# Input in seven plain pieces a batch, outputs stored in row order of their making, one load queue, last chunk in four tiles of 128

## The chip, the cores and the metric

The kernel runs on one core of a Trainium2 chip. Its engines each work through their own list of instructions in order: TensorE (PE, matrix products), VectorE (DVE), ScalarE (ACT), GpSimd (POOL) and SyncE (SP, which only issues transfers). The metric is the device time of one execution in microseconds. Times here are us unless marked ns.

## The reference

Eight batches of 3136 rows with 256 columns go through the real part of a two-dimensional Fourier transform, then through one block with layer norm, two weight matrices, ReLU and a residual.

```python
X = np.fft.fft(np.fft.fft(x, axis=1), axis=2).real          # x: (8, 3136, 256), fp32
mu, var = X.mean(-1), X.var(-1)
xn = (X - mu) / sqrt(var + 1e-6) * g_ln
out = X + np.maximum(xn @ w_ch1, 0) @ w_ch2                 # w_ch1: (256, 1024), w_ch2: (1024, 256)
```

The weights arrive as float64.

## The kernel before

**Fourier transform along the rows.** The input is real, so row k and row 3136-k of the result come from the same two sums, a cosine part a and a sine part b: row k is a+b, row 3136-k is a-b. Only 1569 values of k are computed per batch; k = 0 and k = 1568 have no partner. The length is split as 64 times 49. For each batch, `fold_zw` (L220) adds input rows n and 3136-n into z and w for one of seven pairs of slots, `step1` (L267) multiplies by the 64-point table, ACT copies the product to `s1`, and `store1` (L287) writes it to a scratch tensor in DRAM. `relayout` (L292) reads the scratch back with the other index on the partitions, and `step2` (L308) multiplies by the second table. In batch 0 the folds run on DVE and the products in plain fp32; in batches 1 to 7 the folds run on POOL, two values hi and lo stand for one fp32, and three passes (hi hi, hi lo, lo hi) stand for one product.

**The block.** `step2` leaves the transform along the rows in chunks of 256 values of k (all batches in one line: 49 chunks, the last with 264), as `ck` and its halves `ckh` and `ckl`. The second transform is folded into the first weight matrix. For each chunk there are eight stages s, one per 128 of the 1024 hidden columns: `moe1_a` (L350) makes a and b of the hidden value in PSUM with 6 matmuls; ACT copies a to `asb`; DVE forms `h` = a+b and a-b side by side (512 columns); `moe1_b` (L375) makes the ReLU hi on ACT (`h_hi`) and lo on DVE (`h_lo`); `moe2` (L429) adds 12 matmuls into `acc` for two tiles of 128 rows, both signs. `residual` and its two followers (L454 to L497) make X itself and its variance, `finish` (L514) joins them and `store_out` (L529) writes the rows.

**Order.** PE, ACT, DVE and POOL run in the order in which the program is written, SP too up to the loop. The part ahead of the loop (L719 to L844) is written out by hand; the loop runs `moe1_b(s-1)`, `moe1_a(s)`, late work, `moe2(s-3)`, further work, for s = 6 to 391, with the Fourier work of the next batch put at numbered stages by `add` and `add_late` (L653 to L705).

**Input.** The rows n of a batch go to `x1` by plain loads on 64 partitions each (`load_x`, L182), the rows 3136-n to `x2` by an indirect gather with an index per partition (`gather_x`, L176), issued by POOL. Batch 0 has its own loads on three queues (L725 to L737). Batch 1 is loaded by POOL ahead of the loop (L783 to L785), every further batch in one place of the loop (L691). One partition range of `x2` is cleared by `clear_x`.

**Weights.** Each quarter of a weight matrix is 128 x 512 float64 values; `convert_m`, `convert_z`, `convert_b` (L566 to L590) turn it to fp32 with four DVE instructions and one on ACT, `finish_w1` or `finish_w2` adds one. For w1, `transform_w1` multiplies by the table `tw_s` on PE and `split_w1` makes `w1_hi` on ACT and `w1_lo` on DVE; `split_w2` makes `w2_hi` on ACT and `w2_lo` on POOL.

**Output.** A row k and its partner lie far apart in the output. So `store_out` scatters the a-b half of each tile with an indirect store on POOL (L421) and writes the a+b half with two to four strided stores on SP (`rows`, L540). In the last chunk a third tile of 64 rows, `tail`, holds the 8 columns over 256, both signs (L440 to L444, L518 to L523).

**Stretches without work for PE** are partly filled by matmuls on zeros (`warm_up`, L711).

Of the kernel before, what the change touches and what calls it, by code (L numbers as in the profile page):

```python
# [42 lines left out]
def unit_k(unit):  # L43
    if unit == 0:
        return np.concatenate([64 * np.arange(25), 32 + 64 * np.arange(25)])
    return unit + 64 * np.arange(49)


def runs():

    out, t = [], 0
    for g in range(16):
        for unit in (g, 16 + g):
            if unit == 0:
# [12 lines left out]
def tables():  # L67
# [19 lines left out]
    for g in range(16):  # L87
        for q in range(2):
            k = unit_k(g + 16 * q)
            n = len(k)  # L90
            for par, v in vs:
                al = 2 * np.pi * ((v[:, None] * k) % N) / N
                c, s = np.cos(al), np.sin(al)
                m = len(v)
                for comp in range(2):
                    rows = tab[par, comp, q, :m]
                    if n == 50:
                        half = slice(25 * comp, 25 * comp + 25)
                        rows[:, 0, half], rows[:, 1, half] = c[:, half], s[:, half]
                        tz[2 * par + comp, :m, half] = c[:, half]  # L100
# [19 lines left out]
    tabs["idx"] = index_table()  # L120
# [3 lines left out]
def index_table():  # L124

    idx = np.zeros((128, 2 * NB + 2 * NCH + 1), np.int32)
    rev = 63 - np.arange(64)
    for b in range(NB):
        for j in range(2):
            idx[:64, 2 * b + j] = (b * 64 + rev) * 7 + 5 + j  # L130
            idx[64:, 2 * b + j] = (b * 64 + rev) * 7 + 3 + j
    k = np.concatenate([k0 + 64 * np.arange(n) for _, n, k0 in runs()])
    spare = iter(range(NB * N, ROWS))
    plus = [b * N + i for b in range(NB) for i in k]
    minus = [next(spare) if i in (0, N // 2) else b * N + N - i for b in range(NB) for i in k]
# [9 lines left out]
def tile_kernel(ctx: ExitStack, tc: tile.TileContext, x, g_ln, w1, w2, tu, tab, tz, ty, tw, idx, out):  # L145
# [11 lines left out]
    idx_s = const.tile([128, 2 * NB + 2 * NCH + 1], I32, name="idx_s")  # L157
    idx0 = const.tile([128, 2, 2], I32, name="idx0")
# [7 lines left out]
    x1 = const.tile([128, NS, D], F32, name="x1")  # L166
    x2 = const.tile([128, NS, D], F32, name="x2")
# [3 lines left out]
    spacer = const.tile([128, 1], F32, name="spacer")  # L171

    xv = x.rearrange("b (u v) d -> b u v d", v=49)
    xg = x.rearrange("b (m r) d -> (b m) (r d)", r=7)

    def gather_x(b, j):  # L176
        ix = idx0[:, b, j:j + 1] if b < 2 else idx_s[:, 2 * b + j:2 * b + j + 1]
        nc.gpsimd.indirect_dma_start(
            x2[:, 7 * j:7 * j + 7].rearrange("p s d -> p (s d)"), None, xg,
            bass.IndirectOffsetOnAxis(ap=ix, axis=0))  # L180

    def load_x(b, j, eng=nc.sync):  # L182
        p0 = 7 - 7 * j
        in_order(eng.dma_start(x1[0:64, p0:p0 + 7], xv[b, :, 1 + p0:8 + p0]))
        if p0 == 0:
            in_order(eng.dma_start(x1[64:128, 0:7], xv[b, :, 15:22]))
        else:
            in_order(eng.dma_start(x1[64:128, 7:10], xv[b, :, 22:25]))
            in_order(eng.dma_start(x1[64:128, 10:11], xv[b, :, 0:1]))

    def clear_x(eng=nc.gpsimd):

        eng.memset(x2[64:128, 3:4], 0.0)

    def load_batch(b):
        for j in (1, 0):
            gather_x(b, j)
            load_x(b, j)

    def slots(p0, p1):  # L200
        stop = NS - 1 - p1
        return x1[:, p0:p1], x2[:, NS - 1 - p0:(stop if stop >= 0 else None):-1]
# [17 lines left out]
    def fold_zw(b, i, eng):  # L220
# [5 lines left out]
        a, c = slots(2 * i, 2 * i + 2)  # L226
# [75 lines left out]
    def width(c):  # L302
        return LASTW if c == NCH - 1 else CW

# [3 lines left out]
    def step2(m, part, of=None):  # L308
# [15 lines left out]
        t = b * HALF + base  # L324
        stop = b * HALF + end
        while t < stop:
            c = min(t // CW, NCH - 1)
            n = min(stop, c * CW + width(c)) - t
# [5 lines left out]
            src = ps[:, :, t - b * HALF - base:t - b * HALF - base + n]  # L334
# [10 lines left out]

    def hcols(c):

        return 2 * CW if width(c) == CW else LASTW + 32 + CW

    def moe1_a(s, passes=((0, 1), (1, 0), (0, 0))):  # L350
# [16 lines left out]
        h = hh[s] = work.tile([128, hcols(c)], F32, tag="h", name=f"h{s}", bufs=4)  # L367
        nc.scalar.copy(asb[:, :w], pa)  # L368
        nc.vector.tensor_tensor(out=h[:, :w], in0=asb[:, :w], in1=pb, op=ALU.add)  # L369
        if w > CW:  # L370
            nc.vector.tensor_tensor(out=h[:, w:w + 32], in0=asb[:, w - 32:w], in1=pb[:, w - 32:w],
                                    op=ALU.subtract)
        nc.vector.tensor_tensor(out=h[:, -CW:], in0=asb[:, :CW], in1=pb[:, :CW], op=ALU.subtract)  # L373

    def moe1_b(s):  # L375
        h = hh[s]
        n = hcols(s // 8)
# [7 lines left out]
    def toks(c):  # L385
        t = [(0, 0), (128, 128)]
        if width(c) > CW:
            t.append((LASTW - 32, CW))
        return t

    def tail(i):

        return i == 2

    def previous(engine):
        return next((i for i in reversed(nc.cur_bb.bb.instructions) if i.engine == engine), None)

    stores = []

    def stored(issue, engine):  # L400


        before = previous(engine)
        again = any(i is before for i in stores)
        if again and engine == mybir.EngineType.Pool:
            nc.gpsimd.memset(spacer, 0.0)  # L406
        dma = issue()
# [13 lines left out]
    def scatter(ix, o):  # L421
        stored(lambda: nc.gpsimd.indirect_dma_start(  # L422
            out, bass.IndirectOffsetOnAxis(ap=ix, axis=0), o, None), mybir.EngineType.Pool)

# [4 lines left out]
    def moe2(s, tiles=(0, 1, 2)):  # L429
# [3 lines left out]
        for i, (t0, _) in enumerate(toks(c)):  # L433
            if i not in tiles:
                continue
            if f == 0:
                acc[c, i] = psum.tile([128, 2, D], F32, tag="y" if tail(i) else f"acc{c % 2}",
                                      name=f"acc{c}_{i}", bufs=1 if tail(i) else 2)
            if tail(i):
                for n, (wi, xi) in enumerate(PASSES):  # L440
                    nc.tensor.matmul(acc[c, i][:64, 0], hs[xi][:, t0:t0 + 64], ws[wi][:, f],
                                     start=(f == 0 and n == 0), stop=(f == 7 and n == 2),
                                     skip_group_check=True)
                continue  # L444
            for side in range(2):
                h0 = t0 + side * (hcols(c) - CW)
                for n, (wi, xi) in enumerate(PASSES):
                    nc.tensor.matmul(acc[c, i][:, side], hs[xi][:, h0:h0 + 128], ws[wi][:, f],  # L448
                                     start=(f == 0 and side == 0 and n == 0),
                                     stop=(f == 7 and n == 2), skip_group_check=True)  # L450

    res = {}

    def residual(c, i):  # L454
        t0, _ = toks(c)[i]
        ps = psum.tile([128, 2, 130], F32, tag=f"acc{(c + 1) % 2}", name=f"psy{c}_{i}", bufs=2)
        p = 128
        if tail(i):
            p = 64
            ck = work.tile([128, 2, 2, 32], F32, tag="asb", name=f"dup{c}")  # L460
            for side in range(2):
                nc.scalar.copy(ck[:, :, side], chunk[c][0][:, :, t0:t0 + 32])
            ck = ck.rearrange("p j s t -> p j (s t)")
        else:
            ck = chunk[c][0][:, :, t0:t0 + 128]
# [416 lines left out]
```

## Time and profile before

| what | value |
|---|---|
| median of 3 runs | 1047.05 (1045.32 to 1048.07) |
| profiled execution, its time | 1050.27 |
| profiled execution, first to last instruction | 1048.1 |
| PE busy | 1020.9 (97%), 8319 matmuls |
| DVE busy | 826.4 (79%) |
| ACT busy | 538.4 (51%) |
| POOL busy | 365.6 (35%) |
| bytes moved by DMA | 90.63 MB in 44612 packets, mean 86 GB/s |
| queue of SP (q1) | 35063 packets, 55.33 MB |
| queue of POOL (q0) | 8192 packets, 32.82 MB |

The profiled execution is one execution with the profiler on. A busy PE is not PE at its peak: the end of a matmul is modelled and overlaps the next one, so rates are read from the distance between starts. The view by stretches gives each engine's busy time between two times, the clock granted to PE as a share of full speed, and the share of the 16 DMA engines' time in use. The chain of waits follows the last instruction back to what released it.

### The profile page before, as it was taken

How to read it: one execution, taken by the hardware profiler on the slowest of the kernel's cores; microseconds unless marked ns; L12 is line 12 of the kernel's file. 1: busy time of each engine (PE TensorE's matmuls, PEld its weight loads, DVE VectorE, ACT ScalarE, POOL GpSimd, SP SyncE). 2: the span in 40 equal slices, each digit the busy share in tenths (PEclk: the TensorE clock that was granted, in tenths of full speed). 3: DMA queues.
4: the chain of work that ended last, by engine and by line, in shares of the span. 5: the costliest groups of instructions: out<-in, count | busy, mean ns of one | idle time of the engine just before them, and what ended most of it. 6: DMA issues, size and time to landing. Idle time of an engine off the chain costs nothing.

```text
span 1048.1 us, 22494 instructions
## 1 busy us (share of the span) xinstructions
PE 1020.9 (97%) x8319; PEld 996.3 (95%) x8319; DVE 826.4 (79%) x2200; ACT 538.4 (51%) x1398; POOL 365.6 (35%) x456
## 2 busy tenths in 40 slices
PE   7779999999999999999999999999999999999997
PEld 4479999999999999999999999999999999999997
DVE  3678878887887888887888788787788788788786
ACT  1345555555456545555555645555555554555542
POOL 2327633551255314552245403562234501101101
PEclk9889999999999999999999999999999999999999
DMA  9941370145011631137012631118201230100101
GB/s 230 290 126 32 101 223 23 51 125 180 22 51 51 182 94 41 41 90 223 25 32 66 174 106 35 48 52 222 64 27 46 70 102 22 42 21 26 37 22 43
DMA packets 44612, 90.63 MB, mean 86 GB/s; under 512 B 6984, under 2 KB 33992, under 8 KB 43608
## 3 DMA queue, kind: packets, MB, share of 16 engines
q1 hardware_dynamic: 35063, 55.33, 18.9%
q0 software_dynamic: 8192, 32.82, 10.5%
q8 instruction: 66, 1.08, 0.4%
q10 hardware_dynamic: 1248, 1.05, 0.3%
q14 instruction: 43, 0.34, 0.1%
HBM read 48.74 MB, written 40.44 MB: 85 GB/s over the span
## 4 chain that ended last, share of the span: by engine, by line
PE 77%; issue 12%; DVE 4%; POOL 2%; DMA 1%; ACT 1%; POOLq 0%; DVEq 0%; ACTq 0%
PE acc L448 43%; PE ab L364 22%; PE ps L318 4%; PE psy L467 3%; PE ps L282 3%; POOL out L422 1%; DVE h_lo L381 1%; DMA s<-scratch 1%; DVE h L369 1%; DVE h L373 1%; ACT h_hi L380 0%; DVE ckl L340 0%; DVE st L491 0%; POOL spacer L406 0%; ACT ckh L336 0%
## 5 line engine op out<-in xcount | busy, mean ns | idle before, releaser
L448 PE MATMUL acc<-w_hi,h_lo 128*128 128x256 f32 x1568 | 440.9, 281 | 0.0
L448 PE MATMUL acc<-w_hi,h_hi 128*128 128x256 f32 x1568 | 440.2, 281 | 0.0
L448 PE MATMUL acc<-w_lo,h_hi 128*128 128x256 f32 x1568 | 439.9, 281 | 0.0
L381 DVE SCALAR_TENSOR_TENSOR h_lo<-h,h_hi 128x512 fp32r<-128x512 f32 (+1 forms) x392 | 298.1, 761 | 169.2 <-ACT h_hi L380 167.6
L380 ACT ACTIVATE h_hi<-h 128x512 fp32r<-128x512 f32 (+1 forms) x392 | 250.8, 640 | 264.0 <-DVE h L373 260.8
L448 PEld LDWEIGHTS acc<-w_lo,h_hi 128*128 128x128 f32 x1568 | 295.9, 189 | 0.0
L448 PEld LDWEIGHTS acc<-w_hi,h_lo 128*128 128x128 f32 x1568 | 295.1, 188 | 0.2 <-DVE h_lo L381 0.2
L448 PEld LDWEIGHTS acc<-w_hi,h_hi 128*128 128x128 f32 x1568 | 294.9, 188 | 0.0
L422 POOL DMA_INDIRECT out<-o,idx_s x99 | 99.4, 1004 | 547.6 <-DVE o L524 539.2
L364 PE MATMUL ab<-ckl,w_hi 128*128 128x256 f32 x768 | 221.7, 289 | 10.1 <-DVE ckl L340 8.2
L364 PE MATMUL ab<-ckh,w_lo 128*128 128x256 f32 x768 | 217.0, 283 | 0.3 <-ACT ckh L336 0.3
L364 PE MATMUL ab<-ckh,w_hi 128*128 128x256 f32 x768 | 215.9, 281 | 0.0
L369 DVE TENSOR_TENSOR h<-asb,ab 128x256 f32<-128x256 f32 x384 | 158.2, 412 | 2.6 <-ACT asb L368 2.6
L364 PEld LDWEIGHTS ab<-ckl,w_hi 128*128 128x128 f32 x768 | 145.3, 189 | 14.0 <-DVE ckl L340 8.5
L373 DVE TENSOR_TENSOR h<-asb,ab 128x256 f32<-128x256 f32 x384 | 158.1, 412 | 0.0
L368 ACT COPY asb<-ab 128x256 f32<-128x256 f32 x384 | 139.3, 363 | 28.4 <-PE ab L364 25.7
L364 PEld LDWEIGHTS ab<-ckh,w_lo 128*128 128x128 f32 x768 | 145.7, 190 | 2.8 <-ACT ckh L336 0.5
L364 PEld LDWEIGHTS ab<-ckh,w_hi 128*128 128x128 f32 x768 | 145.9, 190 | 0.0
L245 POOL TENSOR_TENSOR fl<-f,fh 128x512 fp32r<-128x512 f32 x49 | 63.2, 1289 | 67.6 <-ACT fh L239 66.8
L336 ACT CAST ckh<-ps 128x392 fp32r<-128x392 f32 (+49 forms) x112 | 39.6, 355 | 74.8 <-PE ps L318 73.0
L285 ACT COPY s<-ps 128x508 f32<-128x508 f32 x56 | 32.8, 585 | 87.6 <-PE ps L282 66.4
L318 PE MATMUL ps<-tab_s,s 112*128 112x98 f32 (+1 forms) x512 | 65.6, 273 | 1.9 <-issue 1.9
(122 smaller groups left out, 1062.2 us busy)
## 6 DMA issues: line engine op xcount, KB each, us to landing
scratch<-s SPq DMA_DIRECT2D x49, 256.0 KB
s<-scratch SPq DMA_DIRECT2D x7, 1792.0 KB
x<-x SPq DMA_DIRECT2D x19, 448.0 KB
out<-o SPq DMA_DIRECT2D x154, 49.0 KB
w1p_all<-w SPq DMA_DIRECT2D x8, 512.0 KB
out<-o,idx_s POOLq DMA_INDIRECT x99, 3.6
x<-x POOLq DMA_DIRECT2D x3, 448.0 KB, 13.9
x<-x SPq DMA_DIRECT2D x6, 192.0 KB
```

The lines of the kernel that those rows point to most:

```text
L245: nc.gpsimd.tensor_tensor(out=lo, in0=f, in1=hi.bitcast(F32), op=ALU.subtract)
L285: nc.scalar.copy(s[:, :, :, :127], ps[:, :, :, :127])
L318: nc.tensor.matmul(ps[:, h, k0 - base:k1 - base], s2[b][:KP, g, 128 * h:128 * h + 128], tab_s[:, h, k0:k1], start=(h == 0 and g == 2 * j), ...
L336: nc.scalar.copy(hi, src)
L364: nc.tensor.matmul(pt, wt[wi][:, j, fs], ch[xi][:, j, :w], start=(n == 0), stop=(n == 2))
L368: nc.scalar.copy(asb[:, :w], pa)
L369: nc.vector.tensor_tensor(out=h[:, :w], in0=asb[:, :w], in1=pb, op=ALU.add)
L373: nc.vector.tensor_tensor(out=h[:, -CW:], in0=asb[:, :CW], in1=pb[:, :CW], op=ALU.subtract)
L380: nc.scalar.activation(h_hi, h, AF.Relu)
L381: nc.vector.scalar_tensor_tensor(out=h_lo, in0=h, scalar=0.0, in1=h_hi.bitcast(F32), op0=ALU.max, op1=ALU.subtract)
L422: stored(lambda: nc.gpsimd.indirect_dma_start(out, bass.IndirectOffsetOnAxis(ap=ix, axis=0), o, None), mybir.EngineType.Pool)
L448: nc.tensor.matmul(acc[c, i][:, side], hs[xi][:, h0:h0 + 128], ws[wi][:, f], start=(f == 0 and side == 0 and n == 0), stop=(f == 7 and n = ...
```

## The change

It is one rewrite with five parts.

1. **Input.** Numpy lays the input out ahead of the kernel, so that the four rows that slot pair i of partition p needs (two n, two 3136-n) lie together: `x[b, i]` is 128 rows of 4 KB. `load_x(b, i)` is one plain load of 512 KB on SP into `xs[:, i]`. The gathers, the index tables, the three `load_x` forms and `clear_x` go. From batch 2 on, each piece is loaded at its own stage of the loop, two stages behind the fold that frees its place.
2. **Output.** A tile is stored as it stands, both signs of a row side by side, by one store of 128 x 2 KB on SP; numpy puts the rows in order behind the kernel. The scatters on POOL and the strided stores go.
3. **Start.** All loads ahead of the loop stand on SP's queue in the order of their need; the three relayouts of batch 0, the rest of the table and batch 1 come over from POOL's. Of the 40 `warm_up` matmuls 16 go. The conversion of the second and third quarter of w2 moves behind the first stages of the block.
4. **k = 0 and k = 1568** of all batches, 16 values, leave the line of chunks. `step2` puts them aside in `single` (one ACT copy a batch) and `singles` copies them behind the last chunk's 248 other values, which makes 264 again.
5. **Last chunk.** Its 264 a+b and 248 a-b columns are 512, taken as four tiles of 128 (`finish_last`); the third holds 8 columns of the one sign and 120 of the other (`mixed`). The tile of 64 and its matmuls go. Each of the four is stored by itself.

The core of the diff:

```diff
+    def load_x(b, i):
+        in_order(nc.sync.dma_start(xs[:, i], x[b, i]))
...
     def store_out(c, i):
-        o = outs.pop((c, i))
-        if tail(i):
-            scatter(idx_s[:64, -1:], o[:64, 0])
-            return
-        col = 2 * NB + 2 * c + i
-        scatter(idx_s[:, col:col + 1], o[:, 1])
-        rows(o[:, 0], c * CW + toks(c)[i][0])
+        r = (2 * c + i) * CW
+        stored(nc.sync.dma_start(out[r:r + CW].rearrange("(p a) d -> p a d", a=2), outs.pop((c, i))))
...
+            if b + 1 < NB:
+                add(d - 5, load_x, b + 1, i)
...
-        if b + 1 < NB:
-            add(at[-1] - 6, load_batch, b + 1)
...
-            for g0, g1 in ((0, 4), (4, 8), (8, 16)):
-                relayout(0, g0, g1, nc.gpsimd)
-            for j in (1, 0):
-                load_x(1, j, nc.gpsimd)
-                gather_x(1, j)
-            nc.gpsimd.dma_start(tab_s[:, :, gb[8]:], tab[:, :, gb[8]:])
...
+            relayout(0, 0, 4)
+            load_w2(1)
+            relayout(0, 4, 8)
...
+        inverse_std(LC)
+        moe2(last - 3)
+        for i, side in ((0, 0), (1, 0), (0, 1), (1, 1)):
+            for t in (last - 2, last - 1):
+                moe2(t, ((i, side),))
+            finish_last(i, side)
```

How the order moves, at three places. **POOL ahead of the loop**, before: the rows between the stores of batch 0's scratch and the first low half of w2 (`s_0` is the tile that the relayout fills, `x_80` and `x_81` are `x1` and `x2`, already for batch 1).

```order
L289 DMA scratch_151<-s_0_150 128x2x256 x2
L296 DMA s_0_264<-scratch_151 112x1024 x2
L296 DMA s_0_264<-scratch_151 112x2048
L184 DMA x_80<-x 64x1792
L186 DMA x_80<-x 64x1792
L178 DMA x_81<-x,idx_72 128x1792
L184 DMA x_80<-x 64x1792
L188 DMA x_80<-x 64x768
L189 DMA x_80<-x 64x256
L178 DMA x_81<-x,idx_72 128x1792
L786 DMA tab_s<-tab 112x2x784
L594 TENSOR_TENSOR w_lo<-fw_0_316,w_hi 128x512
```

The same place of the changed kernel:

```order
L258 DMA scratch_144<-s_0_143 128x2x256 x2
L525 TENSOR_TENSOR w_lo<-fw_0_299,w_hi 128x512
L525 TENSOR_TENSOR w_lo<-fw_1_356,w_hi 128x512
L741 TENSOR_SCALAR neg<-ty_s 128x1
L525 TENSOR_TENSOR w_lo<-fw_2_430,w_hi 128x512
```

No transfer stands any more between the last scratch store and the low halves of w2 on POOL.

**SP ahead of the loop**, before: the rows from the first load on.

```order
L732 DMA tu_s<-tu 128x388
L734 DMA x_80<-x 64x512
L735 DMA x_80<-x 64x512
L734 DMA x_80<-x 64x1280
L735 DMA x_80<-x 64x1280
L606 DMA w1p_all<-w 128x512
L737 DMA x_80<-x 64x1792
L606 DMA w1p_all<-w 128x512
L739 DMA tw_s<-tw 128x512
```

In the changed kernel (`L171` is a piece of the input, `L534` a quarter of w1, `L539` one of w2, `L265` a relayout):

```order
L655 DMA tu_s<-tu 128x388
L171 DMA xs<-x 128x1024
L534 DMA w1p_all<-w 128x512
L171 DMA xs<-x 128x1024 x3
L534 DMA w1p_all<-w 128x512
L171 DMA xs<-x 128x1024 x3
L534 DMA w1p_all<-w 128x512 x2
L665 DMA tw_s<-tw 128x512
L666 DMA tab_s<-tab 112x2x393
L667 DMA tz_s<-tz 112x50
L539 DMA w1p_all<-w 128x2x256
L265 DMA s_0_260<-scratch_144 112x1024
```

The seven pieces of batch 0 stand as one, three and three. The first relayout now stands behind the first quarter of w2, and the table for w1 behind all of w1 and all of batch 0.

**DVE ahead of the first `ckl`**, before: the rows from the second half of w1's split to the first stage's `h`.

```order
L594 TENSOR_TENSOR w_lo<-psw_300,w_hi 128x512
L587 TENSOR_SCALAR ew_1_335<-ew_1_335 128x512
L589 SCALAR_TENSOR_TENSOR ew_1_335<-w1p_all,ew_1_335 128x512
L640 SCALAR_TENSOR_TENSOR fw_1_337<-fw_1_337,ew_1_335 128x512
L574 TENSOR_SCALAR mw_2_354<-w1p_all 128x512
L576 SCALAR_TENSOR_TENSOR fw_2_355<-w1p_all,mw_2_354 128x512
L587 TENSOR_SCALAR ew_2_353<-ew_2_353 128x512
L589 SCALAR_TENSOR_TENSOR ew_2_353<-w1p_all,ew_2_353 128x512
L340 TENSOR_TENSOR ckl_374<-ps_0_366,ckh_373 128x2x197
L340 TENSOR_TENSOR ckl_374<-ps_1_377,ckh_373 128x2x59
L369 TENSOR_TENSOR h_395<-asb_394,ab_387 128x256
```

In the changed kernel:

```order
L525 TENSOR_TENSOR w_lo<-psw_295,w_hi 128x512
L322 TENSOR_TENSOR ckl_327<-ps_0_319,ckh_326 128x2x195
L322 TENSOR_TENSOR ckl_327<-ps_1_330,ckh_326 128x2x61
L348 TENSOR_TENSOR h_348<-asb_347,ab_340 128x256
L349 TENSOR_TENSOR h_348<-asb_347,ab_340 128x256
L505 TENSOR_SCALAR mw_1_355<-w1p_all 128x512
L507 SCALAR_TENSOR_TENSOR fw_1_356<-w1p_all,mw_1_355 128x512
```

The nine DVE instructions that convert w2's second and third quarter (the first two of the second quarter stand one step above these rows) stood ahead of `ckl` and now stand behind it, between the first stages' `h`.

More of the change, by code (lines that the diff above doesn't have):

```diff
@@ L302, in width, with first_token, singles @@
     def width(c):
-        return LASTW if c == NCH - 1 else CW
+        return MAXW if c == LC else CW
+    def first_token(m):
+        b, j = divmod(m, 8)
+        return b * REG + max(gb[2 * j] - 2, 0)
+    def singles():
+        full, hi, lo = (t[:, :, LASTR:] for t in chunk[LC])
+        nc.scalar.copy(full, single)
+        nc.scalar.copy(hi, single)
+        nc.vector.tensor_tensor(out=lo, in0=single, in1=hi.bitcast(F32), op=ALU.subtract)
     ps2 = {}
@@ L383, in moe1_b, with tiles, stored @@
         hh[s] = (h_hi, h_lo)
[L385 to L407, printed above, removed]
+    def tiles(c):
+        return 4 if c == LC else 2
+    def stored(dma):
         tc.declare_no_dep(dma.ins, group="out", reason="disjoint rows")
         tc.add_to_no_dep_group("out", dma.ins)
-        if engine == mybir.EngineType.SP and not again:
-            tc.keep_in_program_order(dma)
-        stores.append(dma.ins)
+        tc.keep_in_program_order(dma)
     def in_order(dma):
@@ L432, in moe2 @@
         ws = (w2_hi, w2_lo)
[L433 to L438, printed above, removed]
-            if tail(i):
[L440 to L450, printed above, removed]
@@ L452, in tile_kernel @@
-    res = {}
-    def residual(c, i):
[L455 to L465, printed above, removed]
+        for i, side in halves:
+            if f == 0 and side == 0:
+                acc[c, i] = psum.tile([128, 2, D], F32, tag=f"acc{c % 2}", name=f"acc{c}_{i}", bufs=2)
+            h0 = 256 * i + 128 * side if c == LC else 128 * i + 256 * side
+            for n, (wi, xi) in enumerate(PASSES):
+                nc.tensor.matmul(acc[c, i][:, side], hs[xi][:, h0:h0 + 128], ws[wi][:, f],
+                                 start=(f == 0 and side == 0 and n == 0),
+                                 stop=(f == 7 and n == 2), skip_group_check=True)
@@ new lines, in tile_kernel, with mixed @@
+    res = {}
+    def mixed():
+        ck = chunk[LC][0]
+        t = work.tile([128, 2, 128], F32, tag="asb", name="mixed")
+        nc.scalar.copy(t[:, :, 0:8], ck[:, :, MAXW - 8:])
+        nc.scalar.copy(t[:, 0, 8:], ck[:, 0, 0:120])
+        nc.vector.tensor_scalar(out=t[:, 1, 8:], in0=ck[:, 1, 0:120], scalar1=neg, scalar2=None,
+                                op0=ALU.mult)
+        return t
+    def residual(c, i):
+        last = c == LC and i == 2
+        ps = psum.tile([128, 2, 130], F32, tag="y" if last else f"acc{(c + 1) % 2}",
+                       name=f"psy{c}_{i}", bufs=1 if last else 2)
+        t0 = 120 if i == 3 else 128 * i
+        ck = mixed() if last else chunk[c][0][:, :, t0:t0 + 128]
@@ L793, in tile_kernel @@
             load_w2(2)
[L794 removed]
+            relayout(0, 8, 16)
             convert_a("w1_3", w1p[3])
+            split_w1(0)
             convert_b("w1_3")
[L797 to L798 removed]
             finish_w1(3)
             load_w2(3)
[L801 to L802 removed]
+            nc.sync.dma_start(ty_s, ty)
+            nc.sync.dma_start(tab_s[:, :, gb[8]:], tab[:, :, gb[8]:])
+            for i in range(NU):
+                load_x(1, i)
```

347 lines of the change are left out of this document (139 added, 208 removed).

## The prediction

> **What bounds the kernel now.** I read the granted clock and the stretches first, then the chain that ended last, then the waits. The span, and six stretches of it (engine busy times, PE's granted clock, DMA share, GB/s):
>
> ```profile
> span 1048.1 us, 22494 instructions
> ```
>
> ```profile
> 34.00:48.00 14.00, 11.73 (x49) 6.24 (x47) 11.19 (x21) 5.83 (x11) 6.57 (x11) 0.98 0.91 276
> 48.00:56.40 8.40, 0.28 (x2) 0.00 (x0) 3.41 (x5) 0.00 (x0) 3.36 (x4) 0.50 1.02 260
> 56.40:61.00 4.60, 4.46 (x19) 4.20 (x20) 2.13 (x6) 1.92 (x5) 0.00 (x0) 0.50 0.99 256
> 61.00:89.40 28.40, 26.60 (x215) 25.54 (x215) 23.94 (x58) 14.72 (x39) 9.37 (x13) 1.00 0.12 35
> 130.00:1016.00 886.00, 886.00 (x7430) 880.25 (x7429) 715.26 (x1931) 475.03 (x1242) 302.64 (x371) 1.00 0.27 78
> 1041.20:1048.10 6.90, 0.00 (x0) 0.00 (x0) 0.95 (x2) 0.00 (x0) 1.68 (x3) 0.71 0.17 55
> ```
>
> From 130 to 1016 PE is busy 886.00 of 886.00 at full clock while no other engine passes 81%: nothing done to POOL, SP or the queues there can shorten it, only fewer matmuls can. What is left is the start, up to about 89, and the last 6.9. In the start PE does nothing from 48 to 56.4, and the DMA engines are full (1.02). The chain of waits says why (start, length, what):
>
> ```profile
> 39.88 1.12 POOL s L296 x2
> 41.00 9.63 DMA s<-scratch
> ...
> 51.64 1.29 POOL w_lo L594
> ...
> 56.48 2.50 PE ab L364 x10
> ```
>
> POOL issues the relayouts at 39.9, then batch 1's loads, the rest of the table at 51, and only then makes w2's low half at 51.6. Two waits hang on it (longest first, total, times, longest):
>
> ```profile
> PE ab L364 <- DVE ckl L340: 8.2, 1, 8.2
> DVE fw L576 <- POOL w_lo L594: 7.3, 1, 7.3
> ```
>
> DVE, in order, waits for POOL's low half with the conversion of w2's third quarter, `ckl` stands behind that, and PE behind `ckl`. So the stream of stages starts at 56.5, though the first two of its matmuls, which need no `ckl`, ran nine before:
>
> ```profile
> 47.49 0.58 PE L364 MATMUL ab<-ckh,w_lo 128*128 128x256 f32 x1 [0.35 <-ACT ckh L336]
> ```
>
> Its data, then, was there at 47.5. From there on the end follows the start one for one, as long as PE stays full.
>
> POOL's longest wait looks large, and is not on the path:
>
> ```profile
> POOL out L422 <- DVE o L524: 539.2, 74, 17.0
> ```
>
> These 539.2 us are POOL standing before a scatter; the change takes them all away and I cost that at nothing, because PE was full beside them.
>
> **The start, part by part.** Call T the time at which the stages run, 56.5 before. In the changed kernel T is the latest of three lines: the data of batch 0, PE's list, DVE's list. First the loads. Three stretches show what this core's queues move:
>
> ```profile
> 5.00:10.00 5.00, 4.89 (x14) 2.30 (x13) 0.00 (x0) 0.00 (x0) 0.13 (x2) 1.00 0.97 254
> 126.00:130.00 4.00, 4.00 (x32) 3.87 (x31) 3.20 (x11) 2.25 (x5) 3.01 (x3) 1.00 0.99 237
> 134.00:136.00 2.00, 2.00 (x20) 2.00 (x20) 1.35 (x4) 0.82 (x4) 1.53 (x3) 1.00 1.03 416
> ```
>
> 254 at the start and 237 while SP loads `x1` on 64 partitions, 416 while a gather fills all 128. The new pieces are 128 partitions of 4 KB, so they are nearest to the last row; I take 350, with 254 and 416 as ends. The last piece of batch 0 ends 4.9 MB of queue (table 0.2, seven pieces 3.7, two quarters of w1 1.0), `tw_s` ends 6.2 MB. With an estimated 2 us to the first byte they are there at 16 and 20 (14 and 17 at 416; 21.5 and 26.5 at 254, and some 3 later with the first scratch stores between them).
>
> PE's list and DVE's have these prices:
>
> ```profile
> 9.40 2.32 PE L715 MATMUL pw<-warm_h 128*128 128x512 bf16 x10
> ...
> 16.66 0.59 PE L275 MATMUL ps<-zw,tu_s 128*128 128x256 f32 x2
> 17.09 0.59 PE L277 MATMUL ps<-zw,tu_s 128*128 128x256 f32 x2
> ...
> 32.44 3.68 PE L630 MATMUL psw<-gw,tw_s 128*128 128x512 f32 x8
> ```
>
> ```profile
> L576 DVE SCALAR_TENSOR_TENSOR fw<-w1p_all,mw 128x512 f32<-128x512 uint32 x7 | 5.9, 843 | 7.5 <-POOL w_lo L594 7.3
> L589 DVE SCALAR_TENSOR_TENSOR ew<-w1p_all,ew 128x512 int32<-128x512 int32 x7 | 4.8, 692 | 0.2
> L574 DVE TENSOR_SCALAR mw<-w1p_all 128x512 int32<-128x512 int32 x7 | 3.0, 436 | 3.4 <-DMA w1p_all<-w 3.4
> L227 DVE TENSOR_TENSOR zw<-x,x 128x256 f32<-128x256 f32 x7 | 3.0, 431 | 12.6 <-DMA x<-x,idx 11.2 <-DMA x<-x 1.4
> L620 DVE SCALAR_TENSOR_TENSOR gw<-fw,g_s,ew 128x512 f32<-128x512 f32 x4 | 3.0, 751 | 0.1
> ```
>
> PE: the warm-up that stays ends at 11.7. A pair of matmuls starts 0.43 after the one before, a piece is four pairs, 1.72, seven are 12.0; the three small groups for the column ends take about 0.6. So batch 0 is done at 24.4, if each piece is there in time, and the last, due at 22.7, is (at 16; just so at 254). The first half of w1 takes 3.7 more: 28.1. Before, the seven pieces were done only at 32.4, where that row starts.
>
> DVE: until 28 it has slack. Behind 28.1 stand ACT's high half, 0.6 (an estimate, like the 0.4 for `ckl` and the 0.69 for an unlisted pass over 512 columns, from the 0.69 of L589), two low halves 1.4, the rest of the last w1 quarter 1.1 (L589 and one like L574), its finish 0.75, all of the first w2 quarter 2.4 (0.44+0.84+0.42+0.69) and finish 0.7, two low halves 1.4, `ckl`: 36.9.
>
> Data: ACT has copied the last piece at 25.0. Its store is issued by POOL, the relayout now by SP, which waits for it with everything behind on its queue (three quarters of w2, batch 1, all due later). From issue to landing:
>
> ```profile
> scratch<-s POOLq DMA_DIRECT2D x4, 256.0 KB, 7.3
> s<-scratch POOLq DMA_DIRECT2D x2, 448.0 KB, 5.0
> ```
>
> 25.0+7.3+5.0 is 37.3, and the first `step2` and `ckh` add an estimated 1.2: T is 38.5. The store's 7.3 is from full queues; here SP's queue runs dry as it waits, so 4 less is possible, and then DVE's 36.9 decides. T lies between 37 and, with loads at 254 (tables at 29, the same chain behind), 44. The shift is 18.0, between 19.5 and 12.5.
>
> The clock goes to 0.50 in the wait of 48 to 56.4 and is back at 61. PE has an empty stretch before T again, so I keep the half-speed start that T = 56.5 has, at no difference. [...]
>
> **What comes back.** Nine DVE instructions for w2's second and third quarter (2.4+0.7+2.4 = 5.5) now stand between the first stages. From 61 to 89.4 DVE is busy 23.9 of 28.4, the rest is 4.5: they fit almost, but not where the waits are. I take 3 us back, between 0 and 5.5.
>
> **The end.**
>
> ```profile
> L441 PE MATMUL acc<-w_hi,h_lo 128*64 128x256 f32 x8 | 2.2, 280 | 0.0
> ```
>
> ```profile
> 87.96 1.42 PE acc L448 x12
> ...
> 90.25 0.98 PE psy L467 x8
> ```
>
> ```profile
> 1041.20 0.96 DVE L521 SCALAR_TENSOR_TENSOR o<-acc,r,y 32x256 f32<-32x256 f32 x2 [0.19 <-PE acc L441]
> ...
> 1042.44 0.91 POOL L422 DMA_INDIRECT out<-o,idx_s  x1 [0.47 <-DVE o L521]
> ```
>
> The tile of 64 had three such groups of 8, 24 matmuls. At the 0.118 between starts (12 in 1.42 in the chain) that is 2.8 less; the last chunk has one `residual` of 128 more than 128 and 64, 4 matmuls at 0.12: 2.4 net. Behind PE's last matmul stood two DVE passes, a scatter and its landing, 6.9 to the span's end. Now one pass of 0.47 and a plain store of 128 KB: half a pass and POOL's 0.91 go, 1.5 less, between 0.5 and 2.5.
>
> Steady parts that cost nothing: eight copies for `single` on ACT and three small ones (ACT is 54% busy), one store a tile instead of a scatter and two to four strides. On SP a load of the next batch waits for POOL's fold, with stores behind it; three output buffers at two tiles per 20 us (8 stages of 2.51) leave over 20 us.
>
> **Sum.** 18.0 - 3.0 + 2.4 + 1.5 = 18.9. The profiled span of 1048.1 (its own time 1050.27, 3.2 over the median) goes to 1029.2; the median of 1047.05 to 1028. The ends: 19.5+0+2.4+2.5 gives 1022.5; 12.5-5.5+2.4+0.5 gives 1037.
>
> **Rivals.**
> - *Slow loads* (25%): the new pieces run like the row of 254, T is 44. For it: relayouts on 112 partitions stay at 260 in 48 to 56.4. Against it: 416. 12.5-3+2.4+1.5: 1033.5.
> - *The debt* (8%): the conversions and w2's landings take more than their 5.5 back, say 8. For it: DVE's 84% from 61 to 89.4. 18-8+3.9: 1033.
> - *The change does not do what it says* (4%): the single queue is late for every relayout and T stays at 47.5, where the data was before. 9-3+3.9: 1037.
> - *One by one* (3%): SP's queue stops overlapping its transfers, and each of the nine 512 KB loads up to the last piece takes about the 5.0 of the 448 KB relayout: 45 instead of 16, T = 38.5+45-22.7 = 60.8, 4.3 late. -4.3-3+3.9: 1050.5, slower. It decides from 4.6 us a piece. Against it speaks the DMA share of 0.97 from 5 to 10, with loads of SP's queue in flight. [...]
>
> **The numbers.** The forecast has 60%. The range of 1022 to 1037 holds it with its bounds, slow loads and the debt. About 0.3% (3 us) is what a measurement here can tell from no change. Faster 0.95: all but the last rival and misses not listed; same 0.02; slower 0.03.
>
> **What would show it.** In the profile after: the first `moe1_a` matmul near 38 with no wait of 8 on `ckl`; DMA at 330 GB/s or more in the first 15 us; no wait of DVE for POOL's `w_lo`; PE 100% full from some 110 on; the last matmul near 1024 and 5.4 behind it. Wrong, if PE shows gaps in the middle (waits for `step2` or `acc`), if the first stage starts after 48, or if between T and T+50 PE loses over 10 us more than before.

## The result, and the profile after

The changed kernel takes 1030.11 us (median of four executions, 1027.53 to 1031.58), the kernel before, beside it on the same chip, 1046.22. The ratio is 0.984 (95% interval 0.982 to 0.987): 16.1 us faster, where 19 were forecast, and inside the range. The orders that numpy makes ahead of the kernel and behind it are host work, and none of these times holds them. Its profiled execution took 1029.71, with a span of

```profile
span 1027.9 us, 21753 instructions
```

The same stretches as of before (busy PE, PEld, DVE, ACT, POOL; granted clock; DMA share; GB/s): the first loads, batch 0 up to the first stage, the first stages, the next ones, the even part, the end.

```profile
5.00:20.00 15.00, 14.89 (x65) 10.82 (x64) 8.38 (x20) 2.98 (x6) 2.53 (x5) 1.00 1.01 388
24.90:39.80 14.90, 12.34 (x38) 5.58 (x38) 10.92 (x19) 5.91 (x11) 1.99 (x2) 0.89 0.82 232
39.80:53.20 13.40, 9.17 (x56) 8.39 (x56) 10.71 (x23) 6.40 (x16) 1.88 (x2) 0.88 1.02 324
53.20:86.00 32.80, 28.85 (x237) 27.82 (x236) 27.76 (x62) 16.59 (x46) 14.12 (x17) 1.00 0.25 87
130.00:995.00 865.00, 865.00 (x7300) 859.43 (x7299) 692.82 (x1900) 466.26 (x1222) 195.89 (x214) 1.00 0.24 77
1024.40:1027.90 3.50, 0.00 (x0) 0.00 (x0) 0.48 (x1) 0.00 (x0) 0.00 (x0) 1.00 0.28 97
```

Loads run at 388 GB/s (245 in this stretch before), and behind PE's last matmul stand 3.5 instead of 6.9. But PE fills only 9.17 of the 13.40 behind the first stage. Its waits from 24 to 110, longest first:

```profile
PE ab L342 <- DVE h L349: 3.7, 6, 1.5
PE acc L392 <- DVE h_lo L357: 2.8, 2, 2.2
PE psw L558 <- DVE gw L548: 2.1, 1, 2.1
PE psy L415 <- DVE o L466: 1.6, 1, 1.6
PE ps L251 <- DVE ckl L322: 1.1, 1, 1.1
```

No wait of 8 is left, but five sorts of small ones, all for DVE. The chain of waits in these stages (start, length, what) is nearly all DVE's, with the conversions of w2 (L505 to L520, L568) between the stages' own steps:

```profile
39.85 1.07 PE ab L342 x6
...
42.10 0.35 DVE mw L505
42.47 0.69 DVE fw L507
43.17 0.33 DVE h L348
43.83 0.35 DVE ew L518
44.20 0.69 DVE ew L520
44.89 0.60 DVE h_lo L357
45.49 0.33 DVE h L348
46.16 0.61 DVE fw L568
```

The start of each stage's first `moe1_a` matmul, read from the timeline of each kernel, shows where the time went (the kernels in between are the experiments):

| kernel | 0 | 2 | 8 | 16 | 32 | 384 | last matmul ends | span |
|---|---|---|---|---|---|---|---|---|
| before | 47.5 | 59.0 | 74.5 | 96.2 | 141.0 | 1014.2 | 1041.2 | 1048.1 |
| plain_out | 45.2 | 54.3 | 69.9 | 93.0 | 137.1 | 1010.3 | 1037.3 | 1041.6 |
| low_first | 43.5 | 47.4 | 63.0 | 84.6 | 129.5 | 1002.7 | 1029.6 | 1036.5 |
| after | 39.9 | 42.3 | 61.9 | 86.0 | 130.0 | 998.1 | 1024.4 | 1027.9 |
| w2_early | 43.4 | 48.1 | 63.0 | 86.8 | 130.8 | 998.9 | 1025.2 | 1028.8 |
| no_conv | 37.7 | 40.1 | 54.4 | 79.4 | 123.4 | 991.5 | 1017.8 | 1021.4 |
| warm8 | 38.7 | 41.1 | 60.7 | 84.7 | 128.7 | 996.8 | 1023.1 | 1026.7 |
| halves | 48.0 | 50.4 | 70.1 | 94.1 | 138.1 | 1009.5 | 1035.8 | 1039.3 |
| combo | 37.9 | 40.3 | 60.0 | 83.9 | 127.7 | 990.5 | 1015.3 | 1018.8 |

From before to after: 11.0 gained up to stage 32, 5.1 between 32 and 384, 0.6 from there to the last matmul, 3.4 behind it: 20.2, the difference of the spans. The medians differ by 16.1; the missing 4 lie, as far as can be told, in the start of the one profiled execution of before: its own time is 4.05 over the median of 1046.22, and plain_out, which has the same instructions as before until stage 11, reaches stage 8 at 69.9 in its profiled execution, not 74.5.

The 5.1 are a surprise: PE is 100% busy there in both kernels. But a stretch of the same length holds more matmuls. From 200 to 900, before:

```profile
200.00:900.00 700.00, 700.00 (x5857) 694.79 (x5856) 564.36 (x1518) 378.32 (x988) 261.70 (x313) 1.00 0.29 83
```

and after:

```profile
200.00:900.00 700.00, 700.00 (x5898) 695.08 (x5898) 558.52 (x1525) 380.22 (x999) 176.87 (x194) 1.00 0.26 82
```

5898 against 5857. By kind, only `moe2`'s matmuls have changed: from one start to the next 118.0 ns before and 116.8 after (mean of stages 48 to 367, a gap counted as 150 at most; the expectations below give 118.5 and 117.2, from stages 16 to 376 with the waits). `moe1_a`'s stay at 118.7. The 1.2 ns by the 4224 matmuls of `moe2` between stages 32 and 384 are the 5.1 us. And after, the stages alternate: 118.3 in even ones, 115.3 in odd ones.

### The profile page after: what moved, and what is told of

It reads as the page before. It is cut to its first block, busy times and chain, and to the rows that moved or that the text cites. A ratio compares the mean times of both kernels' runs of the same rounds, so it can differ in the third digit from the quotient of the medians.

```text
span 1027.9 us, 21753 instructions
## 1 busy us (share of the span) xinstructions
PE 1008.6 (98%) x8282; PEld 986.0 (96%) x8283; DVE 816.0 (79%) x2195; ACT 539.7 (53%) x1410; POOL 245.0 (24%) x277
## 4 chain that ended last, share of the span: by engine, by line
PE 93%; DVE 5%; ACT 1%; issue 0%; DVEq 0%; ACTq 0%
PE acc L392 51%; PE ab L342 26%; PE ps L298 5%; PE psy L415 4%; PE ps L251 3%; DVE h_lo L357 1%; PE pw L643 1%; DVE h L348 1%; DVE h L349 1%; PE ps L244 1%; PE ps L246 1%; ACT h_hi L356 0%; DVE ew L520 0%; PE psw L558 0%; DVE fw L507 0%
## 5 line engine op out<-in xcount | busy, mean ns | idle before, releaser
L357 DVE SCALAR_TENSOR_TENSOR h_lo<-h,h_hi 128x512 fp32r<-128x512 f32 x392 | 287.9, 735 | 174.1 <-ACT h_hi L356 172.3
L356 ACT ACTIVATE h_hi<-h 128x512 fp32r<-128x512 f32 x392 | 249.8, 637 | 254.2 <-DVE h L349 253.9
L298 PEld LDWEIGHTS ps<-tab_s,s 112*128 112x128 f32 x512 | 63.0, 194 | 0.6 <-PE pw L643 0.6
```

The lines of the kernel that those rows point to most:

```text
L298: nc.tensor.matmul(ps[:, h, k0 - base:k1 - base], s2[b][:KP, g, 128 * h:128 * h + 128], tab_s[:, h, k0:k1], start=(h == 0 and g == 2 * j), ...
L356: nc.scalar.activation(h_hi, h, AF.Relu)
L357: nc.vector.scalar_tensor_tensor(out=h_lo, in0=h, scalar=0.0, in1=h_hi.bitcast(F32), op0=ALU.max, op1=ALU.subtract)
```

## The experiments

Theory: the start gains by an earlier first stage and gives part of it back to DVE; stores and queues in the even part cost nothing, and something else sets `moe2`'s pace. One other thing has moved there. `h_hi` and `h_lo` have four buffers each, and by the built programs' addresses these stand, modulo 128 bytes, at (32, 0), (0, 96), (96, 64), (64, 32) before (2208 apart), and after at 32 or 96 for `h_hi` (2112 apart, odd stages at 32) and at 32 for `h_lo` (2048 apart). w2 is at 96 in both.

**pitch2208**, the old distances in the changed kernel:

```diff
-        h_hi = work.tile([128, n], F32R, tag="h_hi", name=f"h_hi{s}", bufs=4)
-        h_lo = work.tile([128, n], F32R, tag="h_lo", name=f"h_lo{s}", bufs=4)
+        h_hi = work.tile([128, 552], F32R, tag="h_hi", name=f"h_hi{s}", bufs=4)[:, :n]
+        h_lo = work.tile([128, 552], F32R, tag="h_lo", name=f"h_lo{s}", bufs=4)[:, :n]
```

> The changed kernel, but its four buffers of h_hi and of h_lo stand 2208 bytes apart in a partition, as in the kernel before (in the changed kernel 2112 and 2048). Nothing else moves. The mean time from the start of one matmul of the second expert product (acc<-w,h) to the next, between stages 16 and 376 (4320 of them), was 118.5 ns before and 117.2 after, 5.7 us in all. Theory A, the place of these buffers in a partition sets the pace: 118.5 again, and 1030.1 + 5.7, some 1035.5 us. Theory B, the scatters on POOL or the many small stores slowed PE in the kernel before: 117.2 and 1030 us, no change.

1039.42 us, 9.3 over the changed kernel. `moe2` starts every 118.8 ns, `moe1_a` every 119.2. The stretch from 200 to 900:

```profile
200.00:900.00 700.00, 700.00 (x5831) 694.78 (x5830) 552.35 (x1509) 377.09 (x988) 175.50 (x194) 1.00 0.25 81
```

Theory A, and more than it asked for: buffers that PE, ACT and DVE use as in the changed kernel, only in other places, cost 9 us. (The distances are those of before, the pairs of places not quite: (64, 32), (32, 0), (0, 64), (96, 96).)

**pitch2048**, all `h_hi` buffers at 32:

```diff
-        t = work.tile([128, 2, MAXW], F32, tag="h_hi" if i > 3 and b == 0 else "zw",
+        w = CW if i > 3 and b == 0 else MAXW
+        t = work.tile([128, 2, w], F32, tag="h_hi" if i > 3 and b == 0 else "zw",
```

> The changed kernel, but its h_hi buffers stand 2048 bytes apart, not 2112, so that all four have the address of the odd stages' buffers modulo 128 (32; the even stages' have 96). In the changed kernel the matmuls acc<-w,h start 115.3 ns apart in odd stages and 118.3 in even ones. Theory A, addresses: even stages go to 115.3 too, 2350 matmuls by 3.0 ns are 7 us, 1023 us. Theory B, what the other engines do in even and odd stages makes the pattern: it stays, 1030 us.

1025.47 us (ratio to before 0.980, 0.978 to 0.983), 4.6 less than the changed kernel; `moe2` at 115.7 ns, 115.9 in even and 115.5 in odd stages. Theory A, with 4.6 for the expected 7: the odd stages, fast already, lose 0.2 ns, and 1.1 ns over all 4704 matmuls are 5.2. From 200 to 900 PE now does 5931 matmuls instead of 5898:

```profile
200.00:900.00 700.00, 700.00 (x5931) 694.91 (x5930) 563.45 (x1535) 383.19 (x1006) 176.01 (x194) 1.00 0.25 82
```

**plain_out**, before with plain stores and no scatter:

```diff
-            scatter(idx_s[:64, -1:], o[:64, 0])
+            stored(lambda: nc.sync.dma_start(out[2 * NCH * CW:ROWS], o[:64, 0]), mybir.EngineType.SP)
             return
-        col = 2 * NB + 2 * c + i
-        scatter(idx_s[:, col:col + 1], o[:, 1])
-        rows(o[:, 0], c * CW + toks(c)[i][0])
+        r = (2 * c + i) * CW
+        stored(lambda: nc.sync.dma_start(out[r:r + CW].rearrange("(p a) d -> p a d", a=2), o),
+               mybir.EngineType.SP)
```

> The kernel before, with each tile of 128 stored by one plain transfer on SP into rows that follow each other (the rows land in another order), no scatter on POOL and no strided stores. Theory of the prediction, POOL's 539 us before its scatters cost nothing: 1046 us within 1.5, and matmuls acc<-w,h 118.5 ns apart as before. Rival B, the scatters or the small stores slowed PE's reads: 117.2 ns and some 1040.5 us. The end may bring up to 1.5 us in both, as POOL's last scatter is gone.

1043.83 us (ratio 0.998, 0.997 to 0.999), 2.4 less. `moe2` starts every 118.0 ns as before, and the stretch from 200 to 900 holds two more of PE's 5857:

```profile
200.00:900.00 700.00, 700.00 (x5859) 694.88 (x5858) 553.97 (x1518) 379.09 (x987) 192.13 (x214) 1.00 0.27 83
```

So the scatters and small stores cost PE nothing in the even part. This execution also shows the start of the kernel before a second time: its wait for `ckl`, where 8.2 was shown, and the start of the stages in its chain, where 56.48 was shown.

```profile
PE ab L364 <- DVE ckl L340: 5.7, 1, 5.7
```

```profile
51.78 2.50 PE ab L364 x10
```

The 2.4 by which the medians differ are the end: 4.3 from the last matmul to the span's end instead of 7.0, more than the 1.5 allowed.

**low_first**, before with one order on POOL mended:

```diff
-            for j in (1, 0):
-                load_x(1, j, nc.gpsimd)
-                gather_x(1, j)
-            nc.gpsimd.dma_start(tab_s[:, :, gb[8]:], tab[:, :, gb[8]:])
...
             split_w2(0, f)
+            for j in (1, 0):
+                load_x(1, j, nc.gpsimd)
+                gather_x(1, j)
+            nc.gpsimd.dma_start(tab_s[:, :, gb[8]:], tab[:, :, gb[8]:])
             convert_b("w2_1")
```

> The kernel before, with one thing moved: on POOL's list the low half of w2's first quarter stands ahead of the loads of batch 1 and the rest of the table, not behind them. Theory of the prediction: the 8.2 us in which PE waited for ckl are this order alone, and the stages run from 48 to 49 instead of 56.5; with 1 to 3 us coming back behind it 1039 to 1041 us. Rival: the transfers that fill the DMA engines from 41 to 56 hold the start anyway (the relayout, the quarters of w2), T stays at 53 or more, 1043 to 1046 us.

1038.46 us (ratio 0.994, 0.992 to 0.996): 7.7 less. The wait of 8.2 for `ckl` is 0.5 now:

```profile
PE ps L318 <- issue: 2.2, 1, 2.2
PE ab L364 <- DVE h L373: 1.8, 4, 0.8
PE ab L364 <- ACT ckh L336: 0.8, 1, 0.8
PE ab L364 <- DVE ckl L340: 0.5, 1, 0.5
```

In the table it reaches stage 32 at 129.5, half a microsecond ahead of the changed kernel, which at stage 2 is 5 ahead of it. One reordered low half is worth as much to the start as the whole new one.

**no_conv** leaves out ten DVE instructions between the first stages, the nine and the finish of the third quarter (0.7, which stood behind the first stages in both kernels):

```diff
-            convert_a("w2_1", w2p[1])
-            convert_b("w2_1")
-            f = finish_w2(1)
...
-            convert_a("w2_2", w2p[2])
-            convert_b("w2_2")
...
-            f = finish_w2(2)
```

> The changed kernel without the conversion of w2's second and third quarter (nine DVE instructions, 5.5 us, and two of ACT; the first quarter's numbers are written in their place). In the changed kernel the first stage runs at 39.9, but stage 16 only at 86.0, where the kernel before with one load order mended (low_first) has 84.6. Theory A, the debt: DVE's list sets PE's pace up to stage 16, and these 5.5 us are on the path: stage 16 at 81 to 82, 1025 to 1026 us. Theory B, the half clock and the hand-over between PE, ACT and DVE set it: stage 16 within 1 us of 86, 1029 to 1030 us.

1024.00 us, 6.1 less than the changed kernel; stage 16 at 79.4. Of the 6.6 there, 2.1 are gained before the first stage (1.7 of them in a transform that ran faster, see warm8), 4.5 between stages 0 and 16, out of the 6.2 that the ten take on DVE. Its PE waits only 0.8 for `h_lo` (2.8 in the changed kernel):

```profile
PE ab L342 <- DVE h L349: 2.3, 4, 1.4
PE psw L558 <- DVE gw L548: 2.1, 1, 2.1
PE psy L415 <- DVE o L466: 1.6, 1, 1.6
PE acc L392 <- DVE h_lo L357: 0.8, 1, 0.8
```

Theory A: DVE's list is on the path there.

**w2_early** puts these conversions back ahead of the first `ckl`:

```diff
             split_w2(0, f)
+            convert_a("w2_1", w2p[1])
+            convert_b("w2_1")
+            f = finish_w2(1)
+            split_w2(1, f)
+            convert_a("w2_2", w2p[2])
+            convert_b("w2_2")
             warm_up(4, warm_h)
...
-            convert_a("w2_1", w2p[1])
...
-            convert_b("w2_1")
...
-            f = finish_w2(1)
-            split_w2(1, f)
...
-            convert_a("w2_2", w2p[2])
-            convert_b("w2_2")
```

> The changed kernel with the conversions of w2's second and third quarter put back ahead of the first ckl, where the kernel before had them. Theory A, the work is the same and DVE is what bounds the start: the first ckl comes some 5 us later (first full stage at 45 instead of 40.2), stage 16 within 1 us of 86.0, 1029 to 1031 us. Theory B of the prediction, the end follows the first stage and moving them out gained 5.5 for 3 given back: 2 to 3 us slower, 1032 to 1033 us.

1030.96 us, 0.9 more than the changed kernel; stage 2 is 5.9 later than there, stage 16 only 0.8. Theory A: DVE does the same work in either place, and moving it gained 1, not 2.5. (In this profile four matmuls ahead of the first stage took 2.60, in the changed kernel's 3.66, see warm8; with equal clocks the gain could be up to 1 more.)

**halves**, the same pieces in two transfers each:

```diff
-        in_order(nc.sync.dma_start(xs[:, i], x[b, i]))
+        for p in (0, 64):
+            in_order(nc.sync.dma_start(xs[p:p + 64, i], x[b, i, p:p + 64]))
```

> The changed kernel with each piece of x loaded in two transfers of 64 partitions. Theory A of the prediction, such loads run at 237 to 254 GB/s against 332 to 416 with 128 partitions: in the first 15 us some 250 GB/s instead of 330, batch 0 done on PE after 27 instead of 24.9, the first stage some 3 us later; the time up to 3 us more. Theory B, the number of partitions of one transfer does not matter while several are in flight: the same rate, the same start within 0.5 us, 1030 us.

1043.81 us, 13.7 more. The first stretch, and PE's longest wait:

```profile
5.00:20.00 15.00, 14.32 (x58) 9.64 (x57) 6.70 (x17) 2.98 (x6) 2.09 (x3) 1.00 1.02 256
```

```profile
PE psw L559 <- DMA tw_s<-tw: 6.7, 1, 6.7
```

256 GB/s instead of 388, and the DMA engines as full: theory A, but its price was far too low. The packets are no smaller: in this stretch of both traces those of 4 KB carry most of the bytes, and one takes 159 ns (median) in the changed kernel and 264 here. That a transfer is now also only 256 KB was not tested apart. For the table `tw_s`, behind batch 0 and w1 in the queue, PE waits 6.7, the twelve matmuls behind that wait take 7.3 instead of 5.6, and the first stage is at 48.0. Of the 13.7, 8.1 are there by stage 16, and 3.3 come between stages 32 and 384, where `moe2` starts every 117.6 ns; the rest is not in the profiled execution, which took 1041.2. In this kernel's program the four buffers of `h_hi` are taken in another order, two stages running at 32 modulo 128 and two at 96, and `moe2` takes 116.2 to 116.7 ns in the former and 118.3 to 119.2 in the latter: the slow stages are again those with `h_hi` where w2 stands, and no longer the even ones. Why the mean is above the 116.8 of the changed kernel stays open.

**warm8**, eight matmuls on zeros in a wait of 2.1:

```diff
+            warm_up(8, warm_h)
             transform_w1(1, 1)
```

> The changed kernel with eight bf16 matmuls on zeros in PE's wait before the last four matmuls of w1's transform (32.64 us, at half speed: 3.66 us where four took 1.86). Theory A, the clock gate: those four run at full clock, the first stage at 38.0 instead of 39.9. If the end follows the first stage: 1028 us. If DVE's list bounds what follows: stage 16 moves by under 1 us, 1029.5 to 1030 us. Theory B, the half clock has another cause than the idle time: nothing changes but the place of the wait.

1028.04 us. The last four matmuls of the transform, in the timeline of the changed kernel, and then in that of warm8:

```profile
32.64 3.66 PE L558 MATMUL psw<-gw,tw_s 128*128 128x512 f32 x4 [2.12 <-DVE gw L548]
```

```profile
33.15 1.98 PE L558 MATMUL psw<-gw,tw_s 128*128 128x512 f32 x4 [0.40 <-DVE gw L548]
```

1.7 less there, 1.2 less at stages 0, 16 and 32 alike and in the span (2.1 in the medians): theory A, and the end follows. The other executions agree: over the whole span the changed kernel was granted a mean clock of 0.995 to 0.997 in three of its four (1029.71 to 1031.58 us) and 1.000 in one (1027.53), warm8 1.000 in all four (1027.48 to 1028.46). But no_conv waited as long and ran at full speed, and w2_early lay between:

```profile
32.22 1.98 PE L558 MATMUL psw<-gw,tw_s 128*128 128x512 f32 x4 [2.13 <-DVE gw L548]
```

```profile
33.66 2.60 PE L558 MATMUL psw<-gw,tw_s 128*128 128x512 f32 x4 [2.12 <-DVE gw L548]
```

From 32.64 to 36.30 the clock granted in the changed kernel is 0.53. Behind the same wait of 2.1 the four matmuls took 3.66 there, 2.60 in w2_early and 1.98 in no_conv; what decides between them was not shown.

**w2_shift** moves w2 alone, from pitch2048:

```diff
+    const.tile([128, 16], F32, name="pad0")
     w2_hi = const.tile([128, 8, D], F32R, name="w2_hi")
     w2_lo = const.tile([128, 8, D], F32R, name="w2_lo")
+    const.tile([128, 16], F32, name="pad1")
```

> The kernel of pitch2048 with w2's two halves moved by 64 bytes in each partition, from 96 to 32 modulo 128, where h_hi and h_lo stand too; all else keeps its place modulo 128. In pitch2048 the matmuls acc<-w,h start 115.7 ns apart. Theory C, PE reads w2 and h at once and is slowed when both have the same place modulo 128: 118 to 119 ns, 4704 by 2.5 to 3 are 12 to 14 us, some 1038 us. Theory D, only the place of h counts: 115.7 ns and 1025 us.

1039.11 us, 13.6 more than pitch2048; `moe2` at 118.8 ns, in every stage:

```profile
200.00:900.00 700.00, 700.00 (x5835) 694.73 (x5834) 552.92 (x1510) 377.69 (x988) 175.25 (x194) 1.00 0.25 81
```

**shift32** moves all tiles of pitch2048 together:

```diff
+    const.tile([128, 8], F32, name="pad0")
     tu_s = const.tile([128, 388], F32, name="tu_s")
```

> The kernel of pitch2048 with every tile moved by 32 bytes, so that w2 stands at 0 and h at 64 modulo 128 (96 and 32 before) and nearly all others at multiples of 64 as well. Theory C, what counts is the distance of w2 and h modulo 128: 115.7 ns and 1025 us, as in pitch2048. Theory E, reads that begin in the middle of 64 bytes cost more: both products get faster (115.7 and 118.6 ns before), below 115 and 117, 1015 to 1020 us.

1024.99 us; 115.7 and 118.6 ns to the digit of pitch2048:

```profile
200.00:900.00 700.00, 700.00 (x5934) 695.05 (x5933) 563.78 (x1537) 382.98 (x1007) 176.05 (x194) 1.00 0.26 82
```

In these kernels the two runs gave the numbers of theory C: moving all tiles by 32 changed nothing, moving w2 alone 3.1 ns. `moe2` started every 115.7 ns with w2 and `h` 64 apart modulo 128 and every 118.8 with both in the same place. That PE reads the two at once, the theory's reason, was not shown.

**combo** joins pitch2048 and warm8 and treats the last chunk:

```diff
+        own = c == LC and i in (0, 2)
...
-        ps = psum.tile([128, 2, 130], F32, tag="y" if last else f"acc{(c + 1) % 2}",
+        ps = psum.tile([128, 2, 130], F32, tag="y" if own else f"acc{(c + 1) % 2}",
...
+    add_late(8 * LC + 1, lambda: premixed.append(mixed()))
...
-    for i, (r, e, y) in ((2, (1, 2, 2)), (0, (3, 4, 4)), (1, (4, 5, 5)), (3, (4, 5, 6))):
+    for i, (r, e, y) in ((2, (1, 2, 2)), (0, (3, 4, 4)), (1, (4, 5, 5)), (3, (5, 6, 6))):
```

> pitch2048 and warm8 together, and in the last chunk the residuals' three waits of PE (0.4, 1.1 and 0.45 us: for DVE's mixed and for DVE's o) taken away: the mixed columns are made before they are due, the first residual gets a PSUM buffer of its own, the last comes one stage later. If the three add up: 1025.5 - 1.2 - 2.0, some 1022 us. If PE only waits elsewhere in the last chunk: 1024 us.

1020.90 us, ratio to before 0.976 (0.974 to 0.977): faster than both kernels, 9.2 below the changed one, and 1 below the 1022 expected. The two waits for DVE's `o` in the last chunk (1.4) are gone, the one for `mixed` (0.4) has stayed; from stage 384 to the last matmul it takes 24.8 instead of 26.3.

**ck2304** tries the same rule on the first product, from combo:

```diff
-            chunk[c] = (work.tile([128, 2, MAXW], F32, tag="ck", name=f"ck{c}", bufs=3),
+            chunk[c] = (work.tile([128, 2, 288], F32, tag="ck", name=f"ck{c}", bufs=3)[:, :, :MAXW],
...
```

> The kernel of combo with the rule of w2_shift put to use in the other product: the three tiles of a chunk (ck, ckh, ckl) get rows of 288 numbers instead of 264, so that their buffers stand 2304 bytes apart and both halves of each at 32 modulo 128, 64 from w1 (96). In combo these places are mixed (32, 96, and 0 or 64 for the second half) and the matmuls ab<-w,ck start 118.6 ns apart. Theory C, the distance of 64 modulo 128 matters for any pair of operands: 115.7 ns, 2352 by 2.9 are 6.8 us, 1014 us. Theory F, it is something of the second product alone: 118 ns or more, 1020 to 1021 us.

1027.77 us, 6.9 more than combo, where 6.8 less was expected. `moe1_a` stays at 118.4 ns, and `moe2`, whose own operands have not moved, goes from 115.7 to 117.2:

```profile
200.00:900.00 700.00, 700.00 (x5889) 695.02 (x5889) 557.87 (x1524) 379.99 (x998) 175.31 (x194) 1.00 0.25 82
```

Theory F for the first product, and neither theory for the second. Other tiles of the work pool, those of ACT and DVE among them (`ck`, `asb`, the residual's), moved along, so the distance of w2 and `h`, the same at 115.7 and at 117.2, isn't all that goes with the pace. What else does stays open.

## Why the prediction was right, and where it was not

The forecast of 1028 lies 2 below the result, but two of its terms were too large, two too small, and one was not there.

- **T, 38.5 forecast, 39.9 measured, by another line than the one forecast.** Of the three lines, the data were to decide: store 7.3, relayout 5.0, 1.2 for `step2` and `ckh`. In the changed kernel the last scratch store landed 3.0 after its issue, the first relayout 4.6 after its own, and its data lay there at 33.8; the prediction had allowed for such a store and then left T to DVE at 36.9. The chain of waits runs from DVE's conversion of w1's last quarter over the second half of w1's transform, which PE's list in the sum left out, and `step2` takes 2.6:

```profile
31.84 0.76 DVE gw L548
...
32.64 3.66 PE psw L558 x4
36.38 0.83 PE pw L643 x3
37.25 0.69 PE ps L298 x4
...
39.85 1.07 PE ab L342 x6
```

That the number came so close is luck in part: the data line was too long, the rest too short. PE was done with batch 0 at 24.9 (24.4), the loads were faster than the 350 taken (388). The first bytes, estimated at 2 us, moved between 1.50 and 2.00 of the span (40 GB/s in that stretch, 0 ahead of it; 87 and 0 before). 1.7 of the chain is the half speed of w1's last four matmuls, 3.66 for 1.98; of the 16 `warm_up` matmuls that were taken away, six stood in just that place, and the last four took 1.88 behind them. That the wait of 2.1 alone makes the difference is not shown: in no_conv the four took 1.98 behind the same wait.

- **The shift of 18.0** stood on T = 56.5 of one execution, whose own time was 3.2 over the median; the sum was made on that execution and taken from the median. This step failed. Against the profile the shift is 16.6. Another execution of the same start, plain_out's, has a stall of 5.7 instead of 8.2 and runs its stages from 51.8, so of the 16.6 some 5 belong to that one execution.
- **What comes back, 3 forecast,** was 5.6 (16.6 at the first stage, 11.0 at stage 32). The step "they fit almost" took DVE's idle time over 28 us as room; between the first stages there is none. no_conv and w2_early show it: without the ten instructions 4.5 less is lost, and putting the nine back ahead of `ckl` costs only 0.9. Against plain_out's start what is left is 7.2, and low_first has 7.7 by one order on POOL changed.
- **The even part, 0 forecast, 5.1 measured.** "Nothing done to POOL, SP or the queues there can shorten it" holds for the stores (plain_out). "Only fewer matmuls can" was wrong: the change altered tile sizes, with them the places of `h_hi` and `h_lo`, and `moe2` started every 116.8 ns instead of 118.0. It was an accident of the change that it came out faster; pitch2208, with other places alone, gives it back and more (118.8).
- **The tail tile, 2.4 forecast, 0.6 measured.** What is missing is the 1.8 of three waits that were costed at nothing. By stages: from 388 on 2.7 are gained, but 384 to 387 take 2.0 longer, for 1.5 of these waits and two of the four residuals (8 matmuls, 1.0), which stood in 388 and later before, now lie there, and only three of the tail's 24 matmuls and a wait of 0.3 went from there. PE's waits from 990 on in the changed kernel:

```profile
PE psy L415 <- DVE o L466: 1.4, 2, 1.1
PE psy L415 <- DVE mixed L404: 0.4, 1, 0.4
```

- **The end, 1.5 forecast, 3.4 measured.** Half a DVE pass and POOL's issue were counted, but not that the scatter also lands later (3.6 from issue to landing, median, and 1.7 for the 128 KB stores of the changed kernel): plain_out, with both DVE passes left, ends 2.6 earlier.
- **The rivals.** *Slow loads* did not come, and halves shows that such loads exist, with a higher price: the first stage at 48, not 44. *The debt* came halfway, 5.6 for the 3 forecast and the 8 of the rival. *The change does not do what it says* is out with T at 39.9. *One by one* is out: a 512 KB piece takes 4.6 from issue to landing, just the point at which the rival would decide, but the pieces overlap: one alone in 4.6 would be 114 GB/s, and the queue moved 388.

```profile
xs<-x SPq DMA_DIRECT2D x56, 512.0 KB, 4.6
```

Against a start like plain_out's, 7.2 + 5.1 + 0.6 + 3.4 are 16.3, and 16.1 were measured. The number was right partly by luck: the start, forecast at 15 (18 less 3) where 7.2 came against such a start, was made up for by the buffers' places, which nobody had planned, and by the end.

## What to carry to other kernels

An earlier first stage is worth only what the next engine can follow: before moving work behind it, add up each engine's list from there to the point where the kernel runs evenly. Read the base of such a sum from more than one execution, or check it against the median before a difference is taken from it. And when a change alters tile sizes, compare the distance between starts of the same matmuls, since "100% busy" on both sides hides a change of pace (here 700.00 of 700.00 with 5857 matmuls and with 5898).

## What the runs showed of the hardware

- The 128x256 matmuls of `moe2` started 115.7 ns apart with w2 and `h` 64 bytes apart modulo 128 (pitch2048, shift32), and 118.8 with both in the same place (w2_shift): 13.6 us over 4704 of them, from pitch2048 to w2_shift. In ck2304, with w2 and `h` as in combo, they started 117.2 ns apart instead of 115.7, so the places of other tiles went with the pace as well, and which ones was not found.
- With pieces of 512 KB on 128 partitions in one queue, the loads from 5 to 20 us ran at 388 GB/s; with each piece in two transfers of 64 partitions at 256, with the DMA engines counted as full both times (1.01 and 1.02) and 159 and 264 ns for a packet of 4 KB.
- A wait of PE of 2.1 us was followed by four matmuls in 3.66 in the changed kernel (granted clock 0.53), in 3.61 in pitch2048, in 2.60 in w2_early and in 1.98 in no_conv; warm8, with matmuls on zeros in the wait and 0.4 of it left, took 1.98 too.
